# High parts first: the order of chunk 0's matmuls in a DFT and SwiGLU kernel on one core

## The chip, the cores and the metric

The kernel runs on one core of one Trainium2 chip. The metric is device time in microseconds: the median of several runs of one launch, all inputs in HBM at its start and the output in HBM at its end. Beside it there is one profiled execution, from which every duration comes.

## The reference

```python
x = A_x                                            # (1, 2048, 512)
g = sigmoid((x * gate_w).sum(-1, keepdims=True))
a = x @ dft_hid_re.T ;  b = x @ dft_hid_im.T       # 512 x 512
y = dft_seq_re @ a - dft_seq_im @ b                # 2048 x 2048
h = silu(x @ w1) * (x @ w3)                        # 512 x 1376
out = g * y + (1 - g) * (h @ w2)                   # 1376 x 512
```

All of it is in float32.

## The kernel before

**Number format.** A float32 operand is split into two float32r tensors: ScalarE copies it to the high part (`high`, line 108), VectorE subtracts that from the source to get the low part (`low`, line 111). One float32 product is three float32r matmuls on TensorE, high by high, high by low and low by high, all into the same PSUM bank: `mm3`, with its matmul on line 119. The stationary operand is the weight (`w`, called `wa`, `wb` or `a21`), the moving one is x (`xo`, `b12`), 512 columns wide.

**Stages.** First come the gate and up products of SwiGLU, in chunks of 128 of the 1376 columns and two halves of the tokens (a list of 22 items; the names carry the chunk's or item's number). After about 220 us come the transforms and the product with `w2`. Both stages use seven products in place of eight on 2 x 2 blocks, so x is needed as raw blocks B11, B12, B21, B22 and as sums T1 to T4. `sum_xo` (line 204) makes a sum on VectorE, `split_xo` its high and low part. The weights need sums too: `sums_wb` (lines 243 to 246) writes `wu` on VectorE, and `high_wb` and `low_wb` split it into `wb`.

**Chunk 0.** The first chunk is computed by `plain` in eight ordinary block products, since T1 to T4 can't be there yet. `half(i, j, w, x, start)` adds one product to bank `C00`, `C10`, `C01` or `C11`: contraction over 256 rows in two parts, `r = 0` and `r = 1`. Every bank takes two halves, the first with `start`, the second without. Between the steps of `plain` the head issues the splits of what the next step needs: weight form 0 and B11 (in two column halves `q`, so that `r = 0` can begin before the second half is split), `a21`, weight forms 1 and 2 with B21, B12, B22. Before the data come, 11 bfloat16 matmuls on a zero tile (line 393) keep TensorE busy.

**The chunks behind it.** `first1(n)` and `first2(n)` compute products X and Y of item `n` up to three items ahead (lines 280 and 288 take them out of PSUM), and `gate_up(n)` the other five: in the order X (form 4 by T2), Z (5 by T3), X (3 by T1), Z (2 by T4), X (6 by B22), with `first1(n + 3)` ahead of the third and `first2(n + 3)` behind the fourth. Line 362 adds the second X to `u4` on VectorE, line 367 the second Z to `h`. In `gate_up(1)` the product Z by T4 is the first to need T4.

**What sets the order.** Each engine works through a list of instructions, laid out when the program is built. From the loop over `gate_up` on the lists follow the program text (`tc.manual_schedule()`); what is written ahead of that loop, the head with `plain`, is placed by the framework's scheduler, by when it expects operands to be ready. So instructions of the head (the last splits and sums of x, first products of items 1 to 3) stand in the lists between those of `gate_up(1)`. Loads go by SP's queue, stores by POOL's, in the order of issue.

Of the kernel before, what the change touches and what calls it, by code (L numbers as in the profile page):

```python
# [12 lines left out]
P = 128  # L13
# [19 lines left out]
def fnet_swiglu_gate_kernel(  # L33
# [20 lines left out]
    nc = tc.nc  # L54
# [25 lines left out]
    def bank(k, name):  # L80
        return psum.tile([P, 512], F32, tag=f"ps{k}", name=name)
# [35 lines left out]
    def mm3(ps, ah, al, bh, bl, first, last, chain=False):  # L117
        for n, (u, v) in enumerate(((ah, bh), (ah, bl), (al, bh))):
            nc.tensor.matmul(ps, u, v, start=first and n == 0, stop=last and n == 2,  # L119
                             skip_group_check=chain)  # L120
# [191 lines left out]
    def store_h(n, k, h):  # L312

        c, g = ITEMS[n]
        j = min(c % (NP2 - 1) if c < NC - 1 else NP2 - 1, NP2 - 1)
        b = 2 * (NP2 - 1 <= c < NC - 1)
        nc.gpsimd.dma_start(hsp[g, b + k, j // 2, :, j % 2 * 512 : (j % 2 + 1) * 512], h)  # L317
# [78 lines left out]
    def plain(b12, a21):  # L396

        c = {}

        def half(i, j, w, x, start):  # L400
            if start:
                c[i, j] = bank((0, 4, 6, 7)[2 * i + j], f"C{i}{j}")
            for r in range(2):
                sl = slice(r * P, (r + 1) * P)
                mm3(c[i, j], w(0, sl), w(1, sl), x(r, 0), x(r, 1), start and r == 0,
                    not start and r == 1)

        def wa(k):
            return lambda h, sl: WA[0][:, h, k, sl]

        def xb(k):
            return lambda q, h: XO[0][:, h, k, q, :]

        w21 = lambda h, sl: a21[:, h, sl]
        x12 = lambda q, h: b12[:, h, q * 512 : (q + 1) * 512]
        s1 = s1p.tile([P, 512], F32, tag="s1", name="s1_0")
        g1 = u4p.tile([P, 512], F32, tag="u4", name="g1_0")
        h = hp.tile([P, 1024], F32, tag="h", name="h0")
        yield half(0, 0, wa(0), xb(0), True)
        yield half(1, 0, w21, xb(0), True)  # L420
        half(0, 0, wa(1), xb(1), False)
        nc.scalar.activation(s1, c[0, 0], AF.Silu)
        yield half(1, 0, wa(2), xb(1), False)
        nc.vector.tensor_mul(h[:, :512], s1, c[1, 0])
        store_h(0, 0, h[:, :512])
        half(0, 1, wa(0), x12, True)
        yield half(1, 1, w21, x12, True)
        half(0, 1, wa(1), xb(2), False)
        nc.scalar.activation(g1, c[0, 1], AF.Silu)
        half(1, 1, wa(2), xb(2), False)  # L430
        nc.vector.tensor_mul(h[:, 512:], g1, c[1, 1])
        yield store_h(0, 1, h[:, 512:])
# [131 lines left out]
    n = NI - 1 - LOOK  # L564
# [323 lines left out]
    for i, (src, sp, p) in enumerate(late):  # L888
        blk, b = 1 + i // 2, i % 2
        n = (17, 24)[b]  # L890
# [84 lines left out]
```

## Time and profile before

| | us |
|---|---|
| median of 3 runs | 713.85 |
| lowest, highest | 712.9, 715.71 |
| the profiled execution, its time | 715.29 |
| its span, first to last instruction | 713.5 |
| TensorE matmuls busy | 706.0 |
| VectorE busy | 600.8 |
| ScalarE busy | 369.6 |
| mean granted TensorE clock | 0.999 |

The rows of the profile: PE is a TensorE matmul, PEld the load of its weights, which overlaps the matmul before; DVE is VectorE, ACT ScalarE, POOL GpSimd, SP the engine whose queue issues loads. A matmul's end is modelled, and matmuls overlap in the pipeline, so TensorE's gaps are read from the starts of weight loads. In a line of the timeline stand start, duration, engine, line and operation, written and read tiles, shapes, count, and in brackets the idle time ahead of it with what ended it. Tile names stand there without their numbers, and blocks B11 to B22 and sums of x are all `xs_B`, their split parts `xo`.

### The profile page before, as it was taken

The page shows a single profiled execution, that of the slowest core. Times are in us where ns is not written, and L with a number is a line of the kernel's source. Part 1 is how long each engine was busy: PE and PEld are TensorE (multiplying, and loading weights), DVE is VectorE, ACT ScalarE, POOL GpSimd, SP SyncE. Part 2 cuts the span into 40 slices and gives each one's busy share as a digit, 9 for nine tenths or more (in the row PEclk, how much of TensorE's full clock was granted, in tenths as well). Part 3 has the DMA queues.
Part 4 walks back from the last instruction along what each step waited for, and adds up shares of the span by engine and source line. Part 5 has one row for each costly group of instructions (what it writes and reads, how often), then busy time and mean ns, then how long its engine had stood idle before and what let it go on. Part 6 is the DMA issues. An engine that isn't in the chain of part 4 may idle for free.

```text
span 713.5 us, 8596 instructions
## 1 busy us (share of the span) xinstructions
PE 706.0 (99%) x3089; PEld 578.5 (81%) x3089; DVE 600.8 (84%) x729; ACT 369.6 (52%) x477; POOL 67.5 (9%) x122
## 2 busy tenths in 40 slices
PE   9999999999999999999999999999999999999997
PEld 5888888888878887888888888888888888888886
DVE  6979988787668889886999699968997896897985
ACT  6665555655435665454554453644545445455451
POOL 0011111221110010000020001100110010000000
PEclk9999999999999999999999999999999999999999
DMA  7585546589999588812497228915999971773932
GB/s 279 190 297 212 215 186 253 182 318 361 377 326 338 216 227 324 325 60 88 148 341 293 90 71 318 382 40 203 351 418 417 376 251 77 294 266 147 324 119 89
DMA packets 45979, 174.64 MB, mean 245 GB/s; under 512 B 5360, under 2 KB 5488, under 8 KB 42096
## 3 DMA queue, kind: packets, MB, share of 16 engines
q1 hardware_dynamic: 32464, 118.50, 45.7%
q0 software_dynamic: 13184, 55.07, 20.3%
q8 instruction: 24, 0.39, 0.2%
q10 hardware_dynamic: 288, 0.52, 0.2%
q14 instruction: 19, 0.16, 0.1%
HBM read 116.92 MB, written 57.16 MB: 244 GB/s over the span
## 4 chain that ended last, share of the span: by engine, by line
PE 89%; issue 4%; DMA 4%; DVE 0%; ACT 0%; POOL 0%; SPq 0%; POOLq 0%; ACTq 0%
PE P L119 61%; PE X L119 15%; PE Z L119 8%; PE Y L119 4%; DMA B<-cc 1%; DMA wb<-wbsp 1%; PE C L119 1%; DMA p5g<-gs 1%; DMA xs_B<-xt 1%; DVE zo L111 0%; DVE xo L111 0%; ACT zo L108 0%; ACT xo L108 0%; POOL B L656 0%; SPq L221 0%
## 5 line engine op out<-in xcount | busy, mean ns | idle before, releaser
L119 PE MATMUL P<-zo,a 128*128 128x512 f32 x1344 | 306.5, 390 | 0.8 <-DVE zo L111 0.8
L119 PEld LDWEIGHTS P<-zo,a 128*128 128x128 f32 x1344 | 251.8, 188 | 55.5 <-DVE zo L111 3.4
L108 ACT ACTIVATE zo<-B 128x1024 fp32r<-128x1024 f32 (+1 forms) x182 | 188.9, 1045 | 180.8 <-PE P L119 95.0
L111 DVE TENSOR_TENSOR zo<-B,zo 128x1024 fp32r<-128x1024 f32 (+1 forms) x182 | 217.6, 1203 | 52.5 <-ACT zo L108 51.8
L119 PE MATMUL P<-zo,H 128*128 128x512 f32 x468 | 106.2, 389 | 0.0
L119 PEld LDWEIGHTS P<-zo,H 128*128 128x128 f32 x468 | 87.8, 188 | 18.2
L119 PE MATMUL X<-xo,wb 128*128 128x512 f32 x378 | 93.3, 390 | 1.3 <-DMA wb<-wbsp 1.3
L639 DVE TENSOR_TENSOR B<-B,B 128x1024 f32<-128x1024 f32 (+1 forms) x78 | 92.9, 1191 | 0.1
L119 PEld LDWEIGHTS X<-xo,wb 128*128 128x128 f32 x378 | 70.8, 188 | 16.7 <-DMA wb<-wbsp 2.1
L119 PE MATMUL P<-zo,Y 128*128 128x512 f32 x336 | 76.3, 389 | 0.0
L119 PEld LDWEIGHTS P<-zo,Y 128*128 128x128 f32 x336 | 63.1, 188 | 13.1
L317 POOL DMA_DIRECT2D hsp<-h x42 | 23.0, 548 | 128.1 <-DVE h L368 77.1
L119 PE MATMUL X<-xo,wa 128*128 128x512 f32 x126 | 32.3, 389 | 0.0
L119 PE MATMUL Z<-xo,wa 128*128 128x512 f32 x126 | 32.3, 391 | 0.0
L119 PE MATMUL Z<-xo,wb 128*128 128x512 f32 x126 | 32.2, 390 | 0.0
L119 PE MATMUL Y<-xo,wa 128*128 128x512 f32 x126 | 32.2, 389 | 0.0
L362 DVE TENSOR_TENSOR u<-u,X 128x512 f32<-128x512 f32 x21 | 14.4, 687 | 19.2 <-PE X L119 16.8
L851 ACT ACTIVATE zu<-P 128x512 f32<-128x512 f32 x32 | 19.0, 597 | 19.2 <-PE P L119 19.2
L379 ACT ACTIVATE h<-X 128x512 f32<-128x512 f32 x20 | 12.0, 598 | 30.8 <-PE X L119 30.6
L119 PEld LDWEIGHTS Z<-xo,wa 128*128 128x128 f32 x126 | 23.6, 188 | 5.3 <-DVE xo L111 0.4
L119 PEld LDWEIGHTS Z<-xo,wb 128*128 128x128 f32 x126 | 23.7, 188 | 4.9
L119 PEld LDWEIGHTS Y<-xo,wa 128*128 128x128 f32 x126 | 23.7, 188 | 4.9
(134 smaller groups left out, 570.2 us busy)
## 6 DMA issues: line engine op xcount, KB each, us to landing
B<-cc SPq DMA_DIRECT2D x64, 512.0 KB, 6.8
hsp<-h POOLq DMA_DIRECT2D x42, 256.0 KB, 3.6
B<-hsp SPq DMA_DIRECT2D x20, 512.0 KB, 10.3
wbsp<-wb POOLq DMA_DIRECT2D x8, 1024.0 KB, 4.3
wb<-wbsp SPq DMA_DIRECT2D x8, 1024.0 KB, 7.4
B<-zsp SPq DMA_DIRECT2D x16, 512.0 KB, 8.2
H<-w2sp SPq DMA_DIRECT2D x6, 1024.0 KB, 9.3
ws<-w SPq DMA_DIRECT2D x11, 512.0 KB, 7.1
```

The lines of the kernel that those rows point to most:

```text
L108: nc.scalar.activation(hi, src, AF.Copy)
L111: nc.vector.tensor_sub(lo, src, hi.bitcast(F32))
L119: nc.tensor.matmul(ps, u, v, start=first and n == 0, stop=last and n == 2, skip_group_check=chain)
L317: nc.gpsimd.dma_start(hsp[g, b + k, j // 2, :, j % 2 * 512 : (j % 2 + 1) * 512], h)
L362: nc.vector.tensor_add(u4, u4, x)
L379: nc.scalar.activation(g1, x, AF.Silu)
L639: nc.vector.tensor_add(t, t, RAW[blk, b, q][:, :n])
L851: nc.scalar.activation(U[name][:, r], ps[r], AF.Copy)
```

## The change

`half` no longer calls `mm3` once for `r = 0` and once for `r = 1`. It issues the same six matmuls with x's high parts first: weight high and low by x high for `r = 0`, the same for `r = 1`, then weight high by x low for `r = 0` and for `r = 1`. Before, x low of `r = 0` was the second of the six and x low of `r = 1` the fifth. `start` and `stop` stay on the first and last matmul of a bank. Lines below it move by three numbers (line 424 is 427 after, 639 is 642), and chunk 0's matmuls are on line 408 instead of 119.

```diff
         def half(i, j, w, x, start):
             if start:
                 c[i, j] = bank((0, 4, 6, 7)[2 * i + j], f"C{i}{j}")
-            for r in range(2):
-                sl = slice(r * P, (r + 1) * P)
-                mm3(c[i, j], w(0, sl), w(1, sl), x(r, 0), x(r, 1), start and r == 0,
-                    not start and r == 1)
+
+            v = [(slice(r * P, (r + 1) * P), r) for r in range(2)]
+            v = ([(w(h, sl), x(r, 0)) for sl, r in v for h in range(2)]
+                 + [(w(0, sl), x(r, 1)) for sl, r in v])
+            for n, (a, b) in enumerate(v):
+                nc.tensor.matmul(c[i, j], a, b, start=start and n == 0,
+                                 stop=not start and n == len(v) - 1)
```

## The prediction

> **What bounds the kernel now.** I read the page's head and section 1 first, then the table of stages, then the waits of the two TensorE rows, and last the timeline of the first 35 us, where the change lies.
>
> ```profile
> span 713.5 us, 8596 instructions
> PE 706.0 (99%) x3089; PEld 578.5 (81%) x3089; DVE 600.8 (84%) x729; ACT 369.6 (52%) x477; POOL 67.5 (9%) x122
> ```
>
> TensorE is nearly never idle, so the time can move only where it waits. In the timeline one weight load follows the other every 0.227 us (six loads from 28.58 to 29.94, 1.36 / 6); I call that a step. Per stage (columns: busy and count of PE, PEld, DVE, ACT, POOL, then clock, DMA share, GB/s):
>
> ```profile
> 6.00:12.30 6.30, 5.92 (x25) 4.32 (x25) 5.62 (x8) 5.06 (x8) 0.00 (x0) 1.00 1.02 415
> 12.30:24.00 11.70, 11.70 (x53) 9.71 (x52) 11.42 (x15) 9.45 (x12) 1.61 (x3) 1.00 0.42 156
> 24.00:35.00 11.00, 10.99 (x48) 8.75 (x48) 10.27 (x15) 6.17 (x9) 0.18 (x1) 1.00 0.56 212
> ```
>
> The reader is to see two things: in the changed stage (6 to 12.3 us) TensorE has gaps; and in the next 12 us VectorE is as full as TensorE (11.42 of 11.70 us). Two engines there run neck and neck, so work that TensorE gets done sooner helps only if VectorE's list lets it.
>
> The gaps of the changed stage, in the timeline of weight loads:
>
> ```profile
> 5.93 0.19 PEld L119 LDWEIGHTS C<-xo,wa 128*128 128x128 f32 x1 [0.77 <-ACT xo L108]
> 6.66 0.99 PEld L119 LDWEIGHTS C<-xo,wa 128*128 128x128 f32 x5 [0.54 <-DVE xo L111]
> 9.08 0.42 PEld L119 LDWEIGHTS C<-xo,wa 128*128 128x128 f32 x2
> 10.08 2.14 PEld L119 LDWEIGHTS C<-xo,wa 128*128 128x128 f32 x10 [0.58 <-DVE xo L111]
> 12.26 0.19 PEld L119 LDWEIGHTS C<-b,wa 128*128 128x128 f32 x1
> ```
>
> Both waits are for a low part of x from VectorE: that of B11's first half (load at 6.66) and that of B21 (10.08).
>
> The second place is 20 us later, the timeline of VectorE and of the loads around T4, the last sum of x that chunk 1 needs:
>
> ```profile
> 27.86 1.22 DVE L204 TENSOR_TENSOR xs_B<-xs_B,xs_B 128x1024 f32<-128x1024 f32 x1
> 29.00 0.68 DVE L288 TENSOR_TENSOR s<-s,Y 128x512 f32<-128x512 f32 x1
> 29.60 0.42 DVE L243 TENSOR_TENSOR wu<-ws 128x256 f32<-128x256 f32 x1
> 30.05 0.42 DVE L244 TENSOR_TENSOR wu<-wu,ws 128x256 f32<-128x256 f32 x1
> 30.64 1.23 DVE L111 TENSOR_TENSOR xo<-xs_B,xo 128x1024 fp32r<-128x1024 f32 x1 [0.16 <-ACT xo L108]
> 31.79 0.42 DVE L245 TENSOR_TENSOR wu<-ws 128x256 f32<-128x256 f32 x1
> 32.12 0.42 DVE L246 TENSOR_TENSOR wu<-ws,wu 128x256 f32<-128x256 f32 x1
> 32.46 0.68 DVE L362 TENSOR_TENSOR u<-u,X 128x512 f32<-128x512 f32 x1
> ```
> ```profile
> 31.30 0.19 PEld L119 LDWEIGHTS Z<-xo,wa 128*128 128x128 f32 x1
> 31.92 1.01 PEld L119 LDWEIGHTS Z<-xo,wa 128*128 128x128 f32 x5 [0.43 <-DVE xo L111]
> ```
>
> T4's low part is made from 30.64 to 31.87, and product Z of chunk 1 (form 2 by T4) is held until 31.92. From there the loads have no gap until 204 us.
>
> **The change, part by part.** It adds and takes away nothing: 48 matmuls of chunk 0 at the same step, no DMA, vector or scalar instruction more or less, and the order on the POOL and SP queues stays as it was. But the head of the kernel is laid out by the scheduler, so the order of VectorE's, ScalarE's and TensorE's lists after chunk 0 changes too. The order of the built program's instructions, VectorE's around T4, shows it:
>
> ```
> L204 xs0_B21 <- xs0_B21, xs0_B11   (the sum T4)
> L243, L244, L245, L246 wu2         (sums for wb2)
> L362 u4_1 <- u4_1, X1
> L111 xo0 <- xs0_B21, xo0           (T4's low part)
> L111 wb2 <- wu2, wb2
> ```
>
> *Chunk 0 on TensorE.* From 5.93 to 12.26 before: 24 steps, 24 × 0.227 = 5.45, taken 6.33, so 0.88 us are to be had at most. New order: two high matmuls of half 0 (5.93, 6.16); the next two need B11's second high half, which ScalarE ends at 6.40, about 0.06 after the step would be due; the low parts, ready at 6.56 and 7.20, are reached at 6.9 and 7.4 and no longer waited for. B21's high part ends at 8.77, and its step is due at about 8.7: 0.1 lost. Its low part ends at 10.04 and its step, six steps after that, is due at 10.2: no wait. Left over 0.1 to 0.2, gain 0.7 to 0.8: C from b12 starts at about 11.5 instead of 12.26, and TensorE is that much ahead through X and Y of chunks 1 and 2.
>
> *What is late next.* VectorE's list is full from 10.05 on and its work did not shrink. In the new list the low part of ws3 (for X of chunk 3) stands before the subtraction of wb1, and TensorE takes X3 and Y3 before X1 and Z1. Going along the list with the steps of the rows (1.13 for 128x1024, 0.87 for 128x768, 0.60 for 128x512, 0.33 for 128x256), wa3's low part is ready at about 23.4, where X3 is due at 23.4 (a wait of 0.2), and wa4's at 28.9, where X4 is due at 28.5 (a wait of 0.5). So most of the lead is gone by X4.
>
> *T4's low part.* In the new list three instructions that stood behind it stand ahead of it: L245 and L246 of wu2 and L362, which adds product X of chunk 1 to u4. The rest ahead of it is the same set, in another order. Price by the rows' steps: 0.33 + 0.34 + 0.60 (24.39 to 24.99 for the same form) = 1.27. To this comes idle time: the 0.16 ahead of it goes, about 0.27 comes where the addition of Y of chunk 1 now stands earlier than Y is done. T4's low part then starts at 30.64 + 1.27 + 0.1 = 32.0, up to 32.2 with a few waits of VectorE for itself (29.60 to 30.05 is 0.12 longer than 31.79 to 32.12), and ends between 33.25 and 33.45. Z of chunk 1 is the very next product on TensorE after X, nothing can stand in for it, and its second load goes from 31.92 to about 33.4: 1.5 us later. ScalarE's half adds nothing beyond that: T4's high part now stands behind the copy of X4 and ends at about 31.7. L362 waits for X (due at 31.5) and is reached at 31.6; were X later, it would all move with it, so the price has no cheap end below 1.3.
>
> [...]
>
> *After 33.4 us.* All engines' lists are the same again behind T4, loads are issued as buffers come free from TensorE and VectorE, and TensorE has no gap to give the time back before 204 us. So what is lost at Z stays: +1.5 us. The profiled execution (span 713.5, time 715.29) would give 715.0 and 716.8; on the median of the runs, 713.85, it is 715.35. That is 0.2%: a measurement of this kernel tells about 0.5% (3.6 us) from no change, its three runs lie 2.8 us apart.
>
> **The rivals.**
>
> *The lead is kept.* VectorE's later list costs nothing because the few tenths that it waits in 12 to 31 us cover it; T4's low part is ready by 31.1 and the 0.7 to 0.8 of the start stays: 713.1. For it: the table's 0.73 us without VectorE work in 24 to 35. Against: three instructions more ahead of T4 don't fit in there. It decides below 0.5 us of added delay.
>
> *The later waits swallow it.* TensorE waits again at 204 and 212 us for wb:
>
> ```profile
> PEld X L119 <- DMA wb<-wbsp: 2.1, 2, 1.2
> ```
>
> The DMA share is 0.96 from 200 to 230 us; if those loads landed when they do now, 1.5 us of delay would vanish in them: 713.9. Against: the load of wb is issued at 204.78, right as TensorE leaves its buffer, so it moves with TensorE.
>
> [...]
>
> [...]
>
> That the change does not do what it says is no rival: in the built list every half of chunk 0 has its high parts first; only where B21's low part is waited for do matmuls of the other half stand between.
>
> **How the numbers follow.** Forecast (+1.5, T4 late) 0.62; swallowed 0.12; lead kept 0.10; clock falls 0.16. I predict 715.4. Low end: the lead kept, 713.1, less half a microsecond of the runs' own spread, 712.6. High end: the clock case, 717.55, and the same allowance, 718.1. Slower by over 0.5% needs 717.4: the clock case and a rest of it that falls short or lasts twice, together 0.17; faster by over 0.5% needs 710.3, of which no case gives any, 0.03 for what I don't see; within, 0.80.
>
> **What would show it.** Right: C from b12 starts near 11.5; a gap of about 0.5 before X4 goes on; T4's subtraction behind L362 at about 32.1; the load of Z's second matmul near 33.4 and Y, X behind it 1.5 later than before; no new gap from there to 204; the waits for wb as long as before. Wrong: T4's low part before 31.5 (then lead kept), a PEclk below 9 tenths in the second slice (clock), waits for wb gone (swallowed), or a changed tail.

## The result and the profile after

| | before | after |
|---|---|---|
| median of 20 runs, us | 713.73 | 715.79 |
| lowest, highest | 712.9, 715.71 | 714.55, 719.72 |
| the profiled execution, its time | 715.29 | 715.33 |
| its span | 713.5 | 713.6 |

The ratio is 1.0032, 95% interval 1.0021 to 1.0043: 2.06 us slower on the medians, 715.4 was predicted. The two profiled executions differ by 0.1 us only, which looks like no change at all; the first experiment shows why.

The page's head of the kernel after:

```profile
span 713.6 us, 8596 instructions
PE 704.9 (99%) x3089; PEld 577.9 (81%) x3089; DVE 601.2 (84%) x729; ACT 369.1 (52%) x477; POOL 67.5 (9%) x122
```

The timeline of weight loads in the changed stage (start, duration, engine, line, tiles, count, idle time and what ended it):

```profile
5.91 0.30 PEld L408 LDWEIGHTS C<-xo,wa 128*128 128x128 f32 x2 [1.22 <-ACT xo L108]
6.44 0.53 PEld L408 LDWEIGHTS C<-xo,wa 128*128 128x128 f32 x3 [0.23 <-ACT xo L108]
...
7.58 0.99 PEld L408 LDWEIGHTS C<-xo,a 128*128 128x128 f32 x5 [0.15 <-DVE a L111]
8.62 2.68 PEld L408 LDWEIGHTS C<-xo,wa 128*128 128x128 f32 x12
11.34 1.32 PEld L408 LDWEIGHTS C<-b,wa 128*128 128x128 f32 x6
```

Both waits for low parts of x are gone, and 12 matmuls run through where B21's low part was waited for. C from b12 starts at 11.34 instead of 12.26.

The same view 20 us later, and VectorE's list around T4:

```profile
23.44 0.77 PEld L119 LDWEIGHTS X<-xo,wa 128*128 128x128 f32 x4 [0.32 <-DVE wa L111]
...
28.91 0.77 PEld L119 LDWEIGHTS X<-xo,wa 128*128 128x128 f32 x4 [0.61 <-DVE wa L111]
...
31.76 0.19 PEld L119 LDWEIGHTS Z<-xo,wa 128*128 128x128 f32 x1 [0.68 <-ACT xo L108]
33.50 0.99 PEld L119 LDWEIGHTS Z<-xo,wa 128*128 128x128 f32 x5 [1.55 <-DVE xo L111]
```
```profile
28.77 1.22 DVE L204 TENSOR_TENSOR xs_B<-xs_B,xs_B 128x1024 f32<-128x1024 f32 x1
...
31.62 0.69 DVE L362 TENSOR_TENSOR u<-u,X 128x512 f32<-128x512 f32 x1 [0.16 <-PE X L119]
32.23 1.22 DVE L111 TENSOR_TENSOR xo<-xs_B,xo 128x1024 fp32r<-128x1024 f32 x1
```

The lead of 0.92 us at 11.34 turns into a lag of 1.58 us at Z's second load (33.50 against 31.92). T4's subtraction starts at 32.23 behind L362, not at 30.64. That is the predicted chain, within 0.1 us.

### The profile page after: what moved, and what is told of

Its sections match the earlier page's. It is cut to its first block, busy times and chain, and to the rows that moved or that the text cites. A ratio compares the mean times of both kernels' runs of the same rounds, so it can differ in the third digit from the quotient of the medians.

```text
span 713.6 us, 8596 instructions
## 1 busy us (share of the span) xinstructions
PE 704.9 (99%) x3089; PEld 577.9 (81%) x3089; DVE 601.2 (84%) x729; ACT 369.1 (52%) x477; POOL 67.5 (9%) x122
## 4 chain that ended last, share of the span: by engine, by line
PE 90%; issue 5%; DMA 3%; DVE 2%; POOL 0%; ACT 0%; SPq 0%; POOLq 0%; DVEq 0%; ACTq 0%
PE P L119 61%; PE X L119 15%; PE Z L119 8%; PE Y L119 4%; PE C L408 2%; DMA B<-cc 1%; DMA p5g<-gs 1%; DMA xs_B<-xt 1%; DVE xo L111 0%; DVE s L288 0%; DVE zo L111 0%; DVE wb L111 0%; DVE xs_B L204 0%; ACT zo L108 0%; DVE wa L111 0%
## 5 line engine op out<-in xcount | busy, mean ns | idle before, releaser
L362 DVE TENSOR_TENSOR u<-u,X 128x512 f32<-128x512 f32 x21 | 14.4, 688 | 18.3 <-PE X L119 18.3
L119 PEld LDWEIGHTS X<-xo,wa 128*128 128x128 f32 x126 | 23.5, 188 | 5.7 <-DVE wa L111 0.9
```

Source lines behind the costliest of these rows:

```text
L362: nc.vector.tensor_add(u4, u4, x)
```

## The experiments

### Two kinds of execution

The profile of before has the wait for wb at 204 and 212 us, the profile of after has not. To see whether this is the kernels or the executions, both went again unchanged. In all experiments the first number is the ratio to the kernel before, run beside it, with its 95% interval in brackets.

> The kernel before against itself, for a second profile of it. Its runs in the result fall into two groups, 713.4 and 715.4 us, and its first profile (715.29, span 713.5) is of the later group. If the waits of weight loads for wb at 204 and 212 us (2.1 us together) make that group, a profile with a span near 711.5 shows none of them, and one near 713.5 shows both. If they are in every execution, a profile near 711.5 shows them too and differs elsewhere.

> The changed kernel once more, for a second profile. If the late low part of T4 is the loss, Z's second load stands at 33.4 to 33.6 us in every profile, 1.6 us later than before. [...]

Measured: 1.0003 (0.9989 to 1.0016) and 1.0030 (1.0017 to 1.0044). The span of this profile of the kernel before is 711.9, and its waits of weight loads have no row for wb at all. The changed kernel's has one, span 715.3 (engine, tile and line, releaser: us, times, longest):

```profile
core 0 of [0], span 715.3 us
...
PEld X L119 <- DMA wb<-wbsp: 2.2, 1, 2.2
PEld Z L119 <- DVE xo L111: 1.5, 1, 1.5
```

So the wait for wb comes and goes from one execution to the next in either kernel, and is worth some 2 us (1.6 to 2.0 between the spans). Like has to be put beside like (713.3 is from a third comparison, in the last experiment):

| spans of profiled executions, us | without the wait for wb | with it |
|---|---|---|
| before | 711.9 | 713.5 |
| after | 713.6, 713.3 | 715.3 |

The change costs 1.7 and 1.4 us in the first column and 1.8 in the second. The first pair of profiles came one from each column, which hid it.

Z's second load is at 33.50, 33.84 and 33.25 us in the three profiles after. In the second profile of before it is at 32.48, not at 31.92:

```profile
9.39 0.30 PEld L119 LDWEIGHTS C<-xo,wa 128*128 128x128 f32 x2 [0.68 <-ACT xo L108]
10.65 2.12 PEld L119 LDWEIGHTS C<-xo,wa 128*128 128x128 f32 x10 [0.96 <-DVE xo L111]
...
32.48 0.53 PEld L119 LDWEIGHTS Z<-xo,wa 128*128 128x128 f32 x3 [0.43 <-DVE xo L111]
```

There TensorE waited longer for both parts of B21, because B21 came later. So the start of the kernel differs by some tenths of a microsecond from one execution to the next as well, and Z's load is better counted from the moment when ScalarE has B21's high part ready (start and duration of its row together):

| us | B21's high part ready | C from b12 | Z's second load | Z's load counted from B21 |
|---|---|---|---|---|
| before | 8.77 | 12.26 | 31.92 | 23.15 |
| before, again | 9.35 | 12.82 | 32.48 | 23.13 |
| after | 8.53 | 11.34 | 33.50 | 24.97 |
| after, again | 9.01 | 11.74 | 33.84 | 24.83 |
| after, third | 8.38 | 11.13 | 33.25 | 24.87 |

Counted so, the change makes C from b12 about 0.7 us earlier (3.5 us behind B21 before, 2.7 to 2.8 after) and Z's second load 1.7 to 1.8 us later. The spans do not follow Z alone: without the wait for wb Z differs by 0.8 to 1.0 us and the spans by 1.4 to 1.7, so a single pair of spans tells the size to about half a microsecond only.

### A delay alone

Is what is lost at 33 us still lost at the end, or do the waits after 204 us swallow it? The kernel before got nine matmuls nobody reads ahead of Z by T4.

```diff
+        if n == 1:
+            d = bank(4, "idle")
+            for _ in range(9):
+                nc.tensor.matmul(d, WA[1][:, 0, 0, :P], XO[0][:, 0, 0, 0, :], start=True, stop=True)
         prod(z, n, 2, 6, False, True)
```

> The kernel before with 9 extra matmuls into an unused bank ahead of Z by T4: TensorE is kept busy and Z's second matmul starts at 33.8 instead of 32.3, as late as in the changed kernel. Theory (a delay at 33 us is carried to the end): 1.5 us slower, ratio 1.002. Rival (the waits from 204 to 275 us swallow it): ratio 1.000, and the waits for wb shorter than in the kernel before.

Measured: 1.0023 (1.0012 to 1.0035), 715.52 us. Weight loads in its timeline:

```profile
31.65 2.00 PEld L369 LDWEIGHTS idle<-xo,wa 128*128 128x128 f32 x9
33.69 1.32 PEld L119 LDWEIGHTS Z<-xo,wa 128*128 128x128 f32 x6
```

Z's second load is at 33.91, 24.80 us behind B21's high part: a delay of 1.7 us. The span is 713.7 without a wait for wb, 1.8 us over the like profile of before. The delay is carried to the end, and the time's interval excludes 1.000, so the rival that later waits swallow it falls.

### The high parts first in two halves only

```diff
+            if start and j == 0:
+                v = [(slice(r * P, (r + 1) * P), r) for r in range(2)]
...
+            else:
+                for r in range(2):
+                    sl = slice(r * P, (r + 1) * P)
+                    mm3(c[i, j], w(0, sl), w(1, sl), x(r, 0), x(r, 1), start and r == 0,
+                        not start and r == 1)
```

> High parts first in the two halves by B11 alone; the other six halves in the old order. The scheduler then lays the lists behind chunk 0 out as in the kernel before, T4's low part ahead of L245, L246 and L362. Theory (the loss is the late T4; a gain at B11 alone is taken back by the wait for B21's low part at 10.1 us): the first wait of 0.5 us is gone, the wait for B21 grows from 0.5 to 0.8 or 0.9, nothing else moves, ratio 1.000. Rival (the interleaved accumulation into two banks in chunk 0 costs something itself): slower by half of the change's 0.3%, ratio 1.0015.

Measured: 0.9996 (0.9983 to 1.0009). In its timeline the wait for B11's low part is gone, and TensorE stands still for B21 instead:

```profile
9.06 0.30 PEld L119 LDWEIGHTS C<-xo,wa 128*128 128x128 f32 x2 [0.75 <-ACT xo L108]
10.32 2.17 PEld L119 LDWEIGHTS C<-xo,wa 128*128 128x128 f32 x10 [0.96 <-DVE xo L111]
```

The 0.96 can't be read as the gain taken back, since the second profile of before has the same 0.96. Counted from B21's high part (9.01) it can: C from b12 follows after 3.52 us (12.53) and Z's second load after 23.19 (32.20), as in the kernel before. T4's low part stands ahead of L362 there too. The interval reaches to 1.0009, so the rival's 1.0015 is outside it.

### T4 ahead in VectorE's list

T4's sum and split leave the head and go into `gate_up(1)`, where the list follows the text. The rest is the changed kernel.

```diff
         nc.scalar.activation(u2, x, AF.Copy)
+        if n == 1:
+            sum_xo(0, "T4", ST[0, "B21"])
         run(early, n)
         prod(z, n, 5, 5, True, True)
         nc.scalar.activation(u4, z, AF.Copy)
+        if n == 1:
+            split_xo(0, "T4")
...
```

> The changed kernel with T4's sum and split written into the first call of gate_up, so that its low part stands ahead of L243 to L246 and L362 and its high part ahead of the copy of X4. Theory (three instructions ahead of T4's low part make the loss): Z's second load goes from 33.5 to 32.4 us, because VectorE now waits about 1.2 us for the high part between the sum and the subtraction; 1.1 us faster than the changed kernel, ratio to before 1.001. Rival (Z is held by something else): load at 33.5, ratio 1.003.

Measured: 1.0014 (1.0003 to 1.0026). The loads of Z:

```profile
30.97 0.19 PEld L119 LDWEIGHTS Z<-xo,wa 128*128 128x128 f32 x1
32.23 1.01 PEld L119 LDWEIGHTS Z<-xo,wa 128*128 128x128 f32 x5 [1.07 <-DVE xo L111]
```

The wait for T4's low part ends 1.0 to 1.6 us sooner than in the three profiles after. Counted from B21's high part (8.48) the load is at 23.75, which takes away 1.1 of the 1.7 us. What remains is VectorE standing still for T4's high part (1.12 us), and the wait at X4 (0.61 as in the changed kernel). The time agrees but does not decide it: the changed kernel has 1.0017 to 1.0032 in three other comparisons, and the intervals overlap.

### Two additions out of the way

As the last one, and the additions of Y for items 2 and 3, wanted only several products later, go behind T4's sum (`first2` with `False` keeps its addition in `LATER`; `gate1` of the two follows line 362).

```diff
...
-    first2(2)
-    gate1(2)
+    first2(2, False)
...
-    first2(3)
-    gate1(3)
+    first2(3, False)
...
         nc.scalar.activation(u4, z, AF.Copy)
+        if n == 1:
+            high(*xo_parts(0, "T4")[::2])
+            LATER.pop(2)()
+            LATER.pop(3)()
+            low(*xo_parts(0, "T4"))
...
```

> As t4_ahead, and the additions of Y for items 2 and 3 (two instructions on VectorE that nothing needs soon) moved from ahead of T4's sum to between its high and low part. Theory (VectorE's list is the bound from 12 to 32 us, so only work taken out from ahead of T4 keeps the lead of chunk 0): the wait before X4 goes on is gone, Z's second load at 31.2 us with a wait of 0.25, lead of 0.6 kept, ratio to before 0.9992. Rival (the waits from 204 us on take the lead back): Z's load at 31.2, ratio 1.000.

> The kernel of the run named best once more, for a narrower interval (the first gave 0.9990, from 0.9979 to 1.0002). Theory: 0.6 us faster than the kernel before, ratio 0.999. Rival (a draw of how many executions waited for wb): 1.000.

Measured: 0.9990 (0.9979 to 1.0002), then 0.9983 (0.9970 to 0.9996): the lowest times of all runs, 712.41 us in the first and 712.32 in the second. In the second the kernel before had a median of 714.71, where it had 713.4 to 713.9 in the others, so the rival that 0.9983 owes something to the draw of waits for wb is not excluded. Z in the first:

```profile
31.23 0.99 PEld L119 LDWEIGHTS Z<-xo,wa 128*128 128x128 f32 x5 [0.43 <-DVE xo L111]
```

31.23 is 0.69 us ahead of the first profile of before; counted from B21's high part (8.48) it is at 22.75, 0.4 ahead. The wait at X4 is gone, the one at X3 (0.32) is not. Both intervals lie wholly below the three of the changed kernel (lowest end 1.0003), with the same order of matmuls in chunk 0: so it is the lists behind chunk 0 that make the loss, and not the new order itself. To tell whether the order of chunk 0 or the moved additions gain, the same tail ran with the old `half`:

> The same tail (T4 and the additions of Y for items 2 and 3 placed as in best) with the old order of matmuls in chunk 0. Theory (the order of chunk 0 is worth its lead of 0.6 to 0.8 us once nothing behind it takes it back): Z's second load at 31.9 us as in the kernel before, 0.7 later than in best, ratio 1.000. Rival (the moved additions are what gains): load at 31.2, ratio 0.999 as best.

Measured: 0.9994 (0.9979 to 1.0009); Z's second load at 32.05. That is 0.7 to 0.8 us behind best's two profiles (31.23 and 31.35), but B21's high part was ready later too, at 8.88 against 8.48 and 8.63. Counted from it Z's load is at 23.17 against 22.75 and 22.72. So in the trace the order of chunk 0 is worth 0.4 us at Z once the tail lets it through: its lead of 0.7 less the wait at X3. The measured times, 0.9983 against 0.9994 with intervals that overlap, do not decide it.

### Does standing still lower the clock?

Five of the first 20 runs after show a mean granted clock of 0.997 (the others 0.999 or 1.000), at 716.86, 719.02, 719.18, 719.31 and 719.72 us. First the gap was filled with seven matmuls that nobody reads (the edit of the delay, in the changed kernel):

> The changed kernel with 7 extra matmuls into an unused bank just ahead of Z by T4, where TensorE stands still in it; they add 1.6 us of work into a gap of 2.0. Theory (T4 late, and the idle stretch sometimes lowers the clock): Z's second load stays at 33.5, no execution has a clock of 0.997, the runs around 719 are gone and the median falls by about 1 us to 714.8, ratio to before 1.0015 to 1.002. Rival (the runs around 719 come from elsewhere): they stay, median 715.8.

Measured: 1.0036 (1.0023 to 1.0049), no faster than the changed kernel beside it (1.0030), so the expected fall of the median failed. But none of the 11 runs of the changed kernel in this comparison had the low clock either, nor did the filled one: there was nothing to win, and it tells nothing of the five. So the gap was made longer (T4's high part behind `first1(4)`, its low part behind L362 and four repeated additions), and that one filled, with the changed kernel beside both:

```diff
...
         nc.vector.tensor_add(u4, u4, x)
+        if n == 1:
+            for _ in range(4):
+                nc.vector.tensor_add(WU[nw][:, 0], raw[:, 3], raw[:, 2])
+            low(*xo_parts(0, "T4"))
...
```

> The changed kernel with four more (repeated) additions of 128x256 on VectorE ahead of T4's low part, so that TensorE stands still at Z by T4 for 3.5 to 3.8 us instead of 1.5: 2 us more delay, Z's second load at 35.5 to 35.9. Theory (a long enough idle stretch lowers the granted clock): many executions, not only some, show a clock of 0.997 or less, matmuls behind Z run at steps of 0.427 us for some microseconds, and the time is 2 us above the changed kernel in executions without the fall and 3.5 to 4 us above in those with it. Rival (idle time does not move the clock here): clock 1.000 or 0.999 in all, 2 us above.

> As idle_long, with 16 extra matmuls into an unused bank ahead of Z by T4, 3.6 us of work in the same stretch. Z's second load stays at 35.5 to 35.9. Theory: no execution has a clock under 0.999, and the time is the delay alone, 2 us above the changed kernel. Rival: same as idle_long.

> The changed kernel on the same chip as the two. If the idle stretch of 2 us is at the edge of what lowers the clock, some executions here show 0.997 (5 of 20 in the first comparison, 0 of 11 in the second); those are 2 to 4 us above the others. Ratio to before 1.003.

Measured: 1.0090 (1.0074 to 1.0106), 720.0 us; filled 1.0048 (1.0033 to 1.0063), 717.2; the changed kernel 1.0017 (1.0003 to 1.0032), 715.2. The long gap is 4.8 us above the changed kernel, where 3.5 to 4 was expected, the filled one 2.0, as expected. The clock is 0.995 in all six runs of the first and 0.999 or 1.000 in all others of this comparison. Stages of the long gap (columns as before, the clock third from the end), then its loads:

```profile
30.00:34.00 4.00, 2.14 (x9) 1.17 (x7) 3.36 (x9) 2.49 (x3) 0.00 (x0) 0.99 0.36 131
34.00:40.70 6.70, 4.89 (x12) 3.83 (x13) 4.23 (x6) 0.84 (x1) 1.08 (x2) 0.50 0.56 170
40.70:47.00 6.30, 6.30 (x29) 5.20 (x28) 3.68 (x7) 2.87 (x6) 0.55 (x1) 1.00 0.97 358
```
```profile
31.89 0.19 PEld L119 LDWEIGHTS Z<-xo,wa 128*128 128x128 f32 x1 [0.68 <-ACT xo L108]
35.80 1.78 PEld L119 LDWEIGHTS Z<-xo,wa 128*128 128x128 f32 x5 [3.73 <-DVE xo L111]
37.68 2.46 PEld L119 LDWEIGHTS Y<-xo,wa 128*128 128x128 f32 x6
40.24 1.81 PEld L119 LDWEIGHTS X<-xo,wb 128*128 128x128 f32 x7
```

And the filled one:

```profile
31.35 3.60 PEld L377 LDWEIGHTS idle<-xo,wa 128*128 128x128 f32 x16
...
35.91 0.99 PEld L119 LDWEIGHTS Z<-xo,wa 128*128 128x128 f32 x5 [0.73 <-DVE xo L111]
36.95 1.33 PEld L119 LDWEIGHTS Y<-xo,wa 128*128 128x128 f32 x6
38.33 2.68 PEld L119 LDWEIGHTS X<-xo,wb 128*128 128x128 f32 x12
```

Both reach Z at the same time (35.8, 35.9). After 3.7 us of standing still eleven loads take 4.44 us (35.80 to 40.24), filled they take 2.42 (35.91 to 38.33): 2.0 us for the clock (0.50 from 34.0 to 40.7 us in the one, 1.00 in the filled one). The medians differ by 2.8 us (720.0 and 717.2), with six runs each; the wait for wb, 1.4 us in the profile with the long gap and none in the filled one, may be the rest. The eleven follow each other every 0.404 us (4.44 / 11) where 0.427 was expected, the spacing of the loads in the head (1.59 to 5.01 in eight). The mean of 0.99 from 30 to 34 puts the fall of the clock at about 33.9, an estimate, with TensorE busy for 4.9 of the 6.7 us behind 34.0. By that estimate it fell 2.0 us after the last load ahead of the gap (31.89), with 1.9 us of the gap still to come. The changed kernel's own gap, 1.74 us between the loads at 31.76 and 33.50, is 0.3 us shorter than that; its three profiled executions have a mean clock of 1.000.

## Why the prediction was right, and where not

**Chunk 0.** Gain 0.7 to 0.8 predicted; C from b12 started at 11.34 where 11.5 was forecast, 0.92 sooner than in the profile before. That pair flatters it: B21's high part was ready 0.24 us sooner in it (8.53 against 8.77). Counted from B21 the gain is 0.7, as told. The forecast took B21's time from one profile; in the second one after, its high part holds TensorE for 0.39 us where 0.1 was forecast. The wait for B11's second high half is 0.08 in steps (6.44 against 5.91 and two steps), where 0.06 stood; the row's 0.23 counts from the end of the load before.

**What is late next.** X3 waited 0.32 (0.2 forecast), X4 0.61 (0.5), T4's high part ended at 31.71 (31.7). At X4's third load, 28.91 against 29.03 (28.58 and two steps), the lead was down to 0.1 us in this pair.

**T4's low part.** The sum of three steps, 1.27, and idle time put it at 32.0 to 32.2 and Z's second load at 33.4; measured 32.23 and 33.50. VectorE's rows follow the order of the built list: L245, L246 and L362 start at 30.70, 31.04 and 31.62, ahead of it. The added delay was 1.58 us where 1.5 stood, and 1.7 to 1.8 counted from B21. That VectorE's list behind chunk 0 makes the loss is shown by the times, since the changed kernel with that list mended is faster than without it, and the intervals do not overlap. How much of it T4's place alone makes, 1.1 of 1.7 us, is shown in the trace only.

**After 33.4 us.** "+1.5 stays" held: 1.4 to 1.8 us between the spans of like profiles, and 1.8 with a pure delay. What did not come out is the sign "the waits for wb as long as before". These waits were not of the kernel but of the execution, 2.1 us in one profile before and none in the next, and a comparison of the first two profiles alone would have made "swallowed" look true.

**The clock.** The clock case, given 0.16, is a granted clock that drops at the gap at Z. A lower clock came as a second kind of execution rather than as an outcome: 0.997 in 5 runs of 20 in the first comparison, in none of 23 in the two later. Without those five the median after is 715.33, 1.60 over before. They need not be what lies between the sum and the measured 2.06, though: the second comparison, without any such run, gave 2.19 (716.09 against 713.90), and the third 1.62. That the gap at Z causes the low clock was not shown: no profile caught one, the kernel with the longer gap (3.73 us) has 0.995 in all six runs, and the kernel before had single runs at 0.998 (715.28 us) and 0.996 (717.68 us) too. It stays open why it took hold in one comparison and not in two; the two ran on different chips, and on which chip the first ran is not known. No run shows the 2.2 us by which the 717.55 of the clock case is above the forecast's sum: it was the author's estimate, eleven matmuls at the spacing of the head's loads, 0.427 us instead of 0.227, and there the clock's column reads 1.00 (1.2 to 5.9 us). In the long gap, where it reads 0.50, the cost was 2.0. TensorE was busy there for 2.14 of the 4 us from 30 to 34, and in the changed kernel, with 1.00 in the column, for 2.52.

**The size.** 2.06 us on 714 is within the 0.5% said to be hard to tell; 20 runs a side told 0.3% all the same. The forecast of 715.4 lies 0.4 us under the measured 715.79, and the draw of the waits for wb alone moves a median by that much, so the closeness of the hit is partly luck; the chain of waits is not.

## What to carry to other kernels

Where two engines run equally full (here VectorE for 11.42 and TensorE for 11.70 of the 11.7 us from 12.3 to 24.0 in the profile of before), an order that lets one go ahead may only move the wait to the next operand of the other; look for the instructions that the new list puts ahead of that operand, and add their steps. A scheduler that lays out a head can reshuffle all that follows for a change of a few matmuls (here VectorE's list around T4 changed with eight halves in the new order, and not with two), so read the lists of the other engines before costing the edit. And take two or three profiles before reading a difference of 0.2% from one pair: here a wait that comes and goes was as large as the effect (1.6 to 2.0 us between spans, against 1.4 to 1.8), and the arrival of one block of x moved the start by up to a microsecond (B21's high part ready at 8.38 to 9.35 us).

## What the runs showed of the hardware

The eight loads of wb, which SP's queue held until product X was done with their buffer (eight waits, 55.9 us in the first profile of before), had a median time to landing of 7.4 us in the profile of before with the waits and 6.0 in the one without; the core moved 342 and 375 GB/s between 200 and 230 us. B21's high part was ready between 8.38 and 9.35 us in the five profiles of the two kernels; ScalarE, which makes it, stood still for its load for 0.37 us in the first profile of before and for 0.25 in the first after. In the profile of the long gap the clock's column reads 0.99 from 30 to 34 us, 0.50 from 34.0 to 40.7 and 1.00 from 40.7 to 47; the eleven loads behind the gap of 3.7 us took 2.0 us longer than in the filled one, more than half as much as the gap itself.
